# Linear attention and two expert layers: the first batch in a written-out order, its key subtractions and value copies on GpSimd

## The chip, the core and the metric

The kernel runs on one core of a Trainium2 chip. The metric is the device time of one execution in microseconds (us). TensorE (PE) multiplies matrices, VectorE (DVE) and ScalarE (ACT) work on whole tiles, GpSimd (POOL) too, and SyncE (SP) issues the transfers between the chip's main memory and the core's.

## What is computed

```python
# q, k, v: 4 batches x 8 heads x 576 tokens x 64, float32
q_s = exp(q - max over the 64);      q_s = q_s / (sum over the 64 + 1e-09)
k_s = exp(k - max over the tokens);  k_s = k_s / (sum over the tokens + 1e-09)
kv  = einsum("bhsd,bhse->bhde", k_s, v)
att = einsum("bhsd,bhde->bhse", q_s, kv)          # -> x: 2304 tokens x 512
# first expert layer (weights in 64-bit floats)
x   = ((x @ w1) * (x @ w2)) @ w3 @ w_out          # 512 -> 1024 -> 1024 -> 512
# second: 4 experts, weighted by normalised probabilities
out = sum over e of p[:, e] * (relu(x @ e1[e]) @ e2[e])
```

## The kernel before

The tokens run in chunks of 512 columns, `chunks[0]` to `chunks[4]`; a batch has 576 tokens, so chunk 0 is the first 512 tokens of batch 0 and the other 64 belong to chunk 1. The eight heads of a batch are worked in four pairs, in the order `PAIRS = [0, 2, 1, 3]`.

**Attention of one batch.** `load_k`, `load_v`, `load_q` issue the transfers; a pair's keys are a 128x512 tile and a tail of 64 rows. `k_max` takes the maximum over the tokens: three passes on VectorE, a transpose on TensorE, a reduction on VectorE, a matmul that spreads the result over the partitions, and ScalarE's copy `mx`. `k_exp` subtracts `mx` on VectorE (L270) and takes the exponential on ScalarE (L273). `k_v` multiplies keys and values (five matmuls, L285) and makes the block diagonal `bd` of two heads: GpSimd fills it with zeros (L281), ScalarE writes the two blocks, scaled by the reciprocal sums (L299). `load_v` of batch 0 brings the values into a staging tile `vs`, and ScalarE copies them into `vt`, which has a column of ones (L214). The queries come in two tiles `j` of 18 groups of 64: `q_exp` (maximum L308, subtraction L323, exponential L327 with the reordering of rows and heads; for tile (1,1), in `ON_SCALAR`, 18 exponentials of 64 columns with the subtraction and the sum in them, L316), `q_norm` (sum L340, reciprocal, product L343), `q_turn` (three transposes and a copy, three times). `x_stage` multiplies a pair's transposed queries by `bd` in two halves of 288 columns (L368) and splits the result into a high and a low part: ScalarE's copy L384, a matmul with the negative identity L385, ScalarE's copy L389.

**Layer 1.** `ab_step(c, f)`, f from 0 to 7, makes 256 of the 1024 columns of both products of chunk c: two sums of twelve matmuls 128x512 each (three to a pair: high times high L113, high times low L114, low times high L115), called step f below (of chunk 0). The weights come as 64-bit floats and are converted on the chip, one job for each f: two absolute values on ScalarE (`conv_abs`, L144), four passes 128x1024 on VectorE (`conv_rest`, L148, L151, L155, L159), then for each half of the job a high part by a copy on ScalarE (L107) and a low part by a subtraction on VectorE (L108). After that come products of w3 and w_out (`unit`), the rest of the first expert layer, and the second.

**What sets the order.** A scheduler places each engine's instructions. The program gives it the order of the calls: `slot(s)` runs what `put` has listed for slot s by the tables `K_SLOT` and `Q_SLOT` (for batch 0 all in slots 0 to 5; `ab_step(0, f)` is in slot 6 + f). `hold` and `AFTER_JOB` add orders of their own: ("k", 1, 0): 2 means that the first key maximum of batch 1 stands behind the conversion of job 2. SyncE issues all transfers in one row. Psum banks come in pools of two, so a sum has to be read out before the next but one of its pool may start. `keep_busy` issues matmuls that compute nothing needed; the counts behind each pair's transpose, spread and products are `FILL_T`, `FILL_B` and `FILL_V`.

## Time and profile before

| | us |
|---|---|
| median of 3 runs (lowest, highest) | 1153.62 (1153.06, 1154.74) |
| the profiled execution, span from first to last instruction | 1152.2 |
| TensorE busy in it | 1131.9 (98%) |
| VectorE busy | 871.4 (76%) |
| ScalarE busy | 538.3 (47%) |
| GpSimd busy | 50.5 (4%) |

For the profiled execution the span is what is shown; its own time, with what lies around the span, isn't printed beside it. All times in the rows count from the start of the span. The shares are means over 1152 us; the part that the change rewrites is the start, so it is to be read in windows of some microseconds there, engine by engine. An engine's line in a view gives the start, the length, the engine, the line of the code, the operation, out<-in, the size, and in brackets the idle time before it and what ended it. The granted clock (PEclk) is a share of 2.4 GHz.

### The profile page before, as it was taken

How to read it: one execution, taken by the hardware profiler on the slowest of the kernel's cores; microseconds unless marked ns; L12 is line 12 of the kernel's file. 1: busy time of each engine (PE TensorE's matmuls, PEld its weight loads, DVE VectorE, ACT ScalarE, POOL GpSimd, SP SyncE). 2: the span in 40 equal slices, each digit the busy share in tenths (PEclk: the TensorE clock that was granted, in tenths of full speed). 3: DMA queues.
4: the chain of work that ended last, by engine and by line, in shares of the span. 5: the costliest groups of instructions: out<-in, count | busy, mean ns of one | idle time of the engine just before them, and what ended most of it. 6: DMA issues, size and time to landing. Idle time of an engine off the chain costs nothing.

```text
span 1152.2 us, 18837 instructions
## 1 busy us (share of the span) xinstructions
PE 1131.9 (98%) x7091; PEld 1051.2 (91%) x7091; DVE 871.4 (76%) x1432; ACT 538.3 (47%) x986; POOL 50.5 (4%) x74
## 2 busy tenths in 40 slices
PE   7999999999999999999999999999999999999998
PEld 5677877888878889999999999999999999999998
DVE  6986888776558435999989987777779877777777
ACT  4775335755345325655545543334336344344441
POOL 0000032323000000000000000000000000000000
PEclk7999999999999999999999999999999999999999
DMA  9986980899889866877877889777777797777774
GB/s 260 269 330 241 308 203 11 229 323 376 314 290 398 335 261 250 290 284 281 298 265 289 280 313 301 252 246 253 254 249 258 244 307 252 248 246 260 246 247 133
DMA packets 124666, 308.02 MB, mean 267 GB/s; under 512 B 27936, under 2 KB 51488, under 8 KB 124576
## 3 DMA queue, kind: packets, MB, share of 16 engines
q1 hardware_dynamic: 123616, 306.04, 78.2%
q8 instruction: 56, 0.92, 0.3%
q10 hardware_dynamic: 960, 0.79, 0.3%
q14 instruction: 34, 0.28, 0.1%
HBM read 230.24 MB, written 76.55 MB: 266 GB/s over the span
## 4 chain that ended last, share of the span: by engine, by line
PE 88%; DVE 4%; DMA 4%; issue 1%; ACT 1%; SPq 1%; DVEq 0%; ACTq 0%
PE hp L933 30%; PE op L1010 29%; PE ab L113 5%; PE ab L114 5%; PE ab L115 5%; PE y L113 3%; PE y L114 3%; PE y L115 3%; DMA vt<-in_v_dram 2%; PE kv L285 2%; PE xp L368 1%; DMA kr<-in_k_dram 1%; PE W L113 1%; PE W L115 1%; PE W L114 1%
## 5 line engine op out<-in xcount | busy, mean ns | idle before, releaser
L1010 PE MATMUL op<-eg,h 128*128 128x256 f32 x3024 | 379.8, 280 | 0.0
L933 PE MATMUL hp<-t,eg 128*128 128x384 f32 x2016 | 376.6, 336 | 0.9 <-DVE acc L991 0.9
L1010 PEld LDWEIGHTS op<-eg,h 128*128 128x128 f32 x3024 | 373.5, 188 | 0.4 <-PE hp L933 0.3
L933 PEld LDWEIGHTS hp<-t,eg 128*128 128x128 f32 x2016 | 344.6, 188 | 2.5 <-DVE acc L991 1.8
L991 DVE SCALAR_TENSOR_TENSOR acc<-op,prob,acc 128x256 f32<-128x256 f32 (+1 forms) x399 | 197.3, 522 | 42.0 <-PE op L1010 41.9
L107 ACT ACTIVATE h<-blk 128x768 fp32r<-128x768 f32 x168 | 137.9, 842 | 142.3 <-DVE blk L630 108.4
L108 DVE TENSOR_TENSOR h<-blk,h 128x768 fp32r<-128x768 f32 x168 | 156.9, 949 | 24.4 <-ACT h L107 24.3
L916 ACT ACTIVATE blk<-hp 128x384 f32<-128x384 f32 x192 | 90.5, 489 | 142.4 <-PE hp L933 138.9
L920 DVE TENSOR_TENSOR blk<-hp,blk 128x384 f32<-128x384 f32 x144 | 79.1, 554 | 67.7 <-PE hp L933 67.2
L113 PE MATMUL ab<-x,wg 128*128 128x512 f32 (+1 forms) x320 | 120.1, 379 | 2.5 <-ACT bd L299 1.3
L114 PE MATMUL ab<-x,wg 128*128 128x512 f32 (+1 forms) x320 | 118.8, 371 | 0.4 <-ACT x L389 0.4
L115 PE MATMUL ab<-x,wg 128*128 128x512 f32 (+1 forms) x320 | 118.6, 373 | 0.0
L922 ACT ACTIVATE blk<-blk 128x768 f32<-128x768 f32 x72 | 60.6, 845 | 72.7 <-DVE blk L920 71.2
L630 DVE TENSOR_TENSOR blk<-blk 128x768 f32<-128x768 f32 x96 | 91.2, 950 | 0.5
L113 PEld LDWEIGHTS ab<-x,wg 128*128 128x128 f32 x320 | 60.1, 189 | 14.5 <-ACT bd L299 1.7
L114 PEld LDWEIGHTS ab<-x,wg 128*128 128x128 f32 x320 | 60.4, 189 | 11.6 <-ACT x L389 1.9
L115 PEld LDWEIGHTS ab<-x,wg 128*128 128x128 f32 x320 | 60.4, 189 | 10.0
L108 DVE TENSOR_TENSOR eo<-e2r,eo 128x512 fp32r<-128x512 f32 x56 | 41.8, 755 | 21.2 <-ACT eo L107 20.9
L524 DVE TENSOR_TENSOR ah<-ab,ah 128x512 f32<-128x512 f32 (+1 forms) x40 | 25.2, 631 | 39.4 <-PE ab L115 39.2
L114 PE MATMUL y<-h,W 128*128 128x512 f32 x128 | 50.6, 398 | 0.0
L115 PE MATMUL y<-h,W 128*128 128x512 f32 x128 | 50.0, 393 | 0.0
L113 PE MATMUL y<-h,W 128*128 128x512 f32 x128 | 48.9, 402 | 0.0
(103 smaller groups left out, 1060.6 us busy)
## 6 DMA issues: line engine op xcount, KB each, us to landing
eg<-e_t SPq DMA_DIRECT2D x96, 512.0 KB, 4.8
eg<-e_b SPq DMA_DIRECT2D x72, 512.0 KB, 5.2
eg<-e_s SPq DMA_DIRECT2D x68, 512.0 KB, 4.5
eg<-e_a SPq DMA_DIRECT2D x51, 512.0 KB, 4.7
wg<-w SPq DMA_DIRECT2D x44, 512.0 KB, 8.0
f<-in_moe_w_dram SPq DMA_DIRECT2D x32, 512.0 KB, 6.3
e_t<-eo SPq DMA_DIRECT2D x32, 512.0 KB, 7.1
e_s<-eg SPq DMA_DIRECT2D x28, 512.0 KB, 4.3
```

The costliest lines, as they stand in the source:

```text
L107: i = nc.scalar.activation(out=hi, in_=src, func=ACTF.Copy)
L108: j = eng.tensor_tensor(out=lo, in0=src, in1=hi.bitcast(F32), op=ALU.subtract)
L113: nc.tensor.matmul(out=ps, lhsT=w_hi, rhs=r_hi, start=first, stop=False, **kw)
L114: nc.tensor.matmul(out=ps, lhsT=w_hi, rhs=r_lo, start=False, stop=False, **kw)
L115: return nc.tensor.matmul(out=ps, lhsT=w_lo, rhs=r_hi, start=False, stop=last, **kw)
L630: return lambda: nc.vector.tensor_tensor(out=dst, in0=x, in1=y, op=op)
L916: nc.scalar.activation(out=block(name)[:, u], in_=src, func=func)
L920: nc.vector.tensor_tensor(out=x[:, u], in0=src, in1=x[:, u], op=ALU.add)
L922: nc.scalar.activation(out=x, in_=x, func=ACTF.Relu)
L933: nc.tensor.matmul(out=q, lhsT=w[:, sw, kt, P * u:P * u + P], rhs=t[b][:, kt, st], start=new and kt == 0 and i == 0, stop=kt == 1 and i == ...
L991: nc.vector.scalar_tensor_tensor(out=dst, in0=src, scalar=prob[:, T, e:e + 1], in1=dst, op0=ALU.mult, op1=ALU.add,)
L1010: nc.tensor.matmul(out=q[:, c:c + DH], lhsT=g[:, sh, u, P * i:P * i + P], rhs=w[:, sw, u], start=new and u == 0 and j == 0, stop=u == 1 an ...
```

## The change

Batch 0 leaves the tables: its part of `K_SLOT` and `Q_SLOT` is empty, and two new functions write it out. `load_first` issues its transfers: the four key tiles with one transfer of all key tails (`kx`) behind the first, the queries, the values, the values' tails, two jobs of weights. `head` calls small functions (`top`, `spread`, `rest`, `key`, ...) one step at a time, and `seq(engine, inst)` ties each instruction to the one before it on its engine, so that the order is the order of writing. In it

- the subtraction of `mx` from a 128x512 key tile and the copies of the values are on GpSimd (`spread`, `value`); the tails' subtraction stays on VectorE (`rest`);
- the block diagonal is one pass on VectorE, scaled by the reciprocal sum and masked by a tile `same` of zeros and ones (`block`), in place of a fill and two copies on ScalarE;
- queries are exponentiated in place, and the product that normalises them writes them reordered (`norm`); there is one tile `qe`, as before. The same holds for the query tiles of the later batches, (1,1) aside;
- x of chunk 0 is made in matmuls of 512 columns (`out_of`), and the 64 columns of chunk 1 go to one bank `xr` and are split later, behind slot 6 (`x_rest`);
- the conversions of job 0 and the absolute values of job 1 are part of the row (`a_first`, `b_first`), and job 1's four passes are tied to VectorE's row.

Fillers: 78 in place of 43, of which 44 stand behind the last pair's spread. Five jobs are loaded before slot 0. In `AFTER_JOB` batch 1's four keys and its first query tile stand one job earlier. The core of the diff:

```diff
-V_WHOLE = (0,)
-FILL_T, FILL_B, FILL_V = (5, 3, 3, 12), (0, 3, 3, 0), (0, 0, 0, 0)
-K_SLOT = [[0, 0, 0, 0], [6, 7, 8, 9], [30, 32, 34, 36], [46, 47, 48, 50]]
-Q_SLOT = [[2, 2], [6, 8], [30, 34], [46, 48]]
+FILL_T, FILL_B = (5, 3, 3, 3), (0, 3, 3, 44)
+K_SLOT = [[], [6, 7, 8, 9], [30, 32, 34, 36], [46, 47, 48, 50]]
+Q_SLOT = [[], [6, 8], [30, 34], [46, 48]]
 AFTER_JOB = {
-    ("k", 1, 0): 2, ("k", 1, 1): 3, ("k", 1, 2): 4, ("k", 1, 3): 5, ("q", 1, 0): 2, ("q", 1, 1): 3,
+    ("k", 1, 0): 1, ("k", 1, 1): 2, ("k", 1, 2): 3, ("k", 1, 3): 4, ("q", 1, 0): 1, ("q", 1, 1): 3,
     ("in", 2): 13,
 }
...
-        qx = ap_.tile([P, QR, 2, D], F32, tag="qe", name="qe")
-        nc.scalar.activation(
-            out=qx.rearrange("p r h d -> p h r d"), in_=t.rearrange("p (h r) d -> p h r d", h=2),
-            func=ACTF.Exp,
-        )
-        qe[b, j] = qx
+        nc.scalar.activation(out=t, in_=t, func=ACTF.Exp)
+        qe[b, j] = t
...
+    def seq(eng, inst):
+        if eng in chain:
+            after_inst(inst, chain[eng])
+        chain[eng] = inst
+        return inst
...
+            x = kr[i][:, :, 0:KR]
+            seq(G, nc.gpsimd.tensor_tensor(
+                out=x, in0=x, in1=mx.to_broadcast([P, 2, KR, D]), op=ALU.subtract
+            ))
...
+        def value(i):
+            seq(G, nc.gpsimd.tensor_copy(out=vt[0, PAIRS[i]][:, :, 0:KR, 0:D], in_=vs[i]))
...
+            seq(V, nc.vector.scalar_tensor_tensor(
+                out=bd.rearrange("p (h d) -> p h d", h=2),
+                in0=ps[:, 0:2 * D + 2].rearrange("p (h d) -> p h d", h=2)[:, :, 0:D],
+                scalar=rs, in1=same.rearrange("p (h d) -> p h d", h=2),
+                op0=ALU.mult, op1=ALU.mult,
+            ))
...
+            seq(T, nc.tensor.matmul(
+                out=ps, lhsT=st[i]["bd"], rhs=qT[hp % 2][:, hp // 2, 0:CH], start=True, stop=True
+            ))
...
+        top(0), spread(0)
+        top(1), rest(0), key(0)
+        top(2), spread(1)
+        top(3), rest(1), spread(2), spread(3), rest(2), rest(3)
+        key(1), key(2)
+        less(0), query(0), key(3)
+        less(1), query(1)
+        value(0), value(1), value(2), value(3)
+        kv(0), kv(1)
+        total(0), block(0), kv(2), norm(0)
+        total(1), block(1)
+        a_first(0)
+        turn(0, 0), turn(0, 1), kv(3), turn(0, 2)
+        norm(1)
+        out_of(0), out_of(1), out_rest(0), out_rest(1)
+        block(2), block(3), b_first(0)
+        high(0), turn(1, 0), minus_high(0), high(1), turn(1, 1), low(0), minus_high(1)
+        turn(1, 2), low(1)
+        out_of(2), out_of(3), out_rest(2), out_rest(3)
+        high(2), minus_high(2), b_first(1), high(3), minus_high(3), b_first(2)
+        low(2), low(3), a_first(1)
...
-    for i in range(AB0):
-        if i == 3:
-            convert(1)
-        slot(i)
+    load_first()
+    head()
+    load_to(1 + AHEAD)
     for i in range(AB0):
         slot(i)
+    put(after, AB0, x_rest)
```

The order of three places, word for word (a row is the line, the operation, out<-in, the size and how many in a row). First ScalarE, where the steps 3 and 4 of layer 1 are served; before, `wg_736` and `wg_739` are the high parts of step 4's weights, `mx_678` is the maximum of batch 1's third pair, and L316 are the 18 exponentials of query tile (1,1):

```order
L107 ACTIVATE wg_634<-f32_545 128x512
L107 ACTIVATE wg_637<-f32_545 128x512
L523 ACTIVATE ah_680<-ab_681 128x512
L260 ACTIVATE mx_678<-mt_673 128x128
L107 ACTIVATE wg_736<-f32_627 128x512
L107 ACTIVATE wg_739<-f32_627 128x512
L144 ACTIVATE f32_729<-f64_472 128x512 x2
L316 ACTIVATE qe_643,qs_644<-qr_461,qm_640 128x64 x18
L299 ACTIVATE bd_709<-kv_711,rs_717 64x64 x2
```

Now (step 4's are `wg_746` and `wg_749`, the third pair's maximum is `mx_688`, the exponentials are L296, the key exponentials L255):

```order
L761 ACTIVATE ah_690<-ab_772 128x512
L337 ACTIVATE qT_618<-qt_629 128x2x192
L296 ACTIVATE qe_653,qs_654<-qr_455,qm_650 128x64 x18
L255 ACTIVATE ek_673<-kr_447 128x2x4x64
L255 ACTIVATE ek_673<-kr_447 64x128
L242 ACTIVATE mx_688<-mt_683 128x128
L106 ACTIVATE wg_746<-f32_637 128x512
L106 ACTIVATE wg_749<-f32_637 128x512
L279 ACTIVATE bd_719<-kv_721,rs_727 64x64 x2
```

The 18 exponentials stand ahead of the high parts of step 4's weights and of the third maximum, behind which they stood before.

Second VectorE, where it goes from batch 0's queries to the weights of job 0. Before (`f32_324` is job 0, `f32_327` job 1, `qe_258` the second query tile):

```order
L148 TENSOR_SCALAR f32_327<-f32_327 128x1024
L159 SCALAR_TENSOR_TENSOR f32_324<-f64_134,f32_324 128x1024
L295 RECIPROCAL rs_294<-rs_294 128x1
L151 TENSOR_SCALAR f32_327<-f32_327 128x1024
L340 TENSOR_REDUCE qs_345<-qe_258 128x18
L292 TENSOR_SCALAR rs_307<-kv_301 128x1
L155 SCALAR_TENSOR_TENSOR f32_327<-f64_312,f32_327 128x1024
L108 TENSOR_TENSOR wg_334<-f32_324,wg_334 128x512
L108 TENSOR_TENSOR wg_337<-f32_324,wg_337 128x512
L341 TENSOR_SCALAR qs_345<-qs_345 128x18
```

Now (job 0 is `f32_332`; `qe_359` the second query tile, `bdg_150` holds the block diagonals, `kv_316` and `kv_346` are the third and fourth pair's products):

```order
L529 TENSOR_TENSOR qe_359<-qr_123,qs_326 128x2x9x64
L488 TENSOR_SCALAR rs_368<-kv_316 128x1
L491 RECIPROCAL rs_368<-rs_368 128x1
L493 SCALAR_TENSOR_TENSOR bdg_150<-kv_316,rs_368,bdg_150 128x128
L488 TENSOR_SCALAR rs_372<-kv_346 128x1
L491 RECIPROCAL rs_372<-rs_372 128x1
L493 SCALAR_TENSOR_TENSOR bdg_150<-kv_346,rs_372,bdg_150 128x128
L147 TENSOR_SCALAR f32_332<-f32_332 128x1024
L150 TENSOR_SCALAR f32_332<-f32_332 128x1024
L154 SCALAR_TENSOR_TENSOR f32_332<-f64_144,f32_332 128x1024
L158 SCALAR_TENSOR_TENSOR f32_332<-f64_144,f32_332 128x1024
L107 TENSOR_TENSOR wg_413<-f32_332,wg_413 128x512
```

Jobs 0 and 1 stood between the query's passes; now the query's and the blocks' passes are done first, and job 1 comes after job 0's low parts.

Third TensorE, up to layer 1's first matmul (L113 before, L112 now). Before:

```order
L355 MATMUL qt_362<-ident_75,qe_253 128x128 x3
L355 MATMUL qt_367<-ident_75,qe_253 128x128 x3
L355 MATMUL qt_372<-ident_75,qe_253 128x128 x3
L368 MATMUL xp_393<-qT_361,bd_260 128x288
L285 MATMUL kv_301<-vt_148,ek_245 128x130 x5
L368 MATMUL xp_408<-qT_361,bd_273 128x288
L368 MATMUL xp_395<-qT_361,bd_260 128x288
L368 MATMUL xp_410<-qT_361,bd_273 128x288
L385 MATMUL xp_393<-x0_0_397,nident_76 128x288
L385 MATMUL xp_395<-x0_0_397,nident_76 128x224
L113 MATMUL ab_514<-x0_0_397,wg_334 128x512
```

Now:

```order
L560 MATMUL xr_365<-qT_335,bdg_150 128x64 x2
L541 MATMUL qt_383<-ident_75,qe_359 128x128 x3
L572 MATMUL xp_361<-x0_0_380,nident_76 128x512
L541 MATMUL qt_391<-ident_75,qe_359 128x128 x3
L572 MATMUL xp_363<-x0_2_389,nident_76 128x512
L541 MATMUL qt_398<-ident_75,qe_359 128x128 x3
L551 MATMUL xp_404<-qT_382,bdg_150 128x512
L551 MATMUL xp_406<-qT_382,bdg_150 128x512
L560 MATMUL xr_365<-qT_382,bdg_150 128x64 x2
L572 MATMUL xp_404<-x0_1_410,nident_76 128x512
L112 MATMUL ab_507<-x0_0_380,wg_413 128x512
```

The matmuls of 288 columns have become some of 512 and 64, the first matmuls of all four pairs' x stand ahead of the first `ab`, and the transposes of the second query tile (`qe_359`) are among them; before they stood behind it.

## Rows read from the trace of the kernel before

**Rows 1.** Page, head and part 1: span; busy time, share, instructions.

```profile
span 1152.2 us, 18837 instructions
...
PE 1131.9 (98%) x7091; PEld 1051.2 (91%) x7091; DVE 871.4 (76%) x1432; ACT 538.3 (47%) x986; POOL 50.5 (4%) x74
```

**Rows 2.** Windows: length, busy PE, PEld, DVE, ACT, POOL (instructions), PEclk, DMA share, GB/s.

```profile
10.00:20.00 10.00, 6.43 (x30) 4.88 (x30) 5.66 (x11) 3.45 (x6) 0.00 (x0) 0.66 1.08 281
20.00:30.00 10.00, 8.18 (x33) 6.39 (x34) 9.90 (x19) 7.76 (x18) 0.97 (x3) 0.67 1.11 336
...
40.00:50.00 10.00, 8.86 (x43) 6.30 (x42) 10.00 (x20) 8.38 (x22) 0.41 (x2) 1.00 1.15 253
50.00:60.00 10.00, 10.00 (x49) 8.24 (x48) 10.00 (x19) 5.36 (x13) 0.00 (x0) 1.00 1.11 356
```

**Rows 3.** Timeline, TensorE: start, length, line, operation; idle before, releaser.

```profile
10.74 0.49 PE L127 MATMUL busy<-ones 128*128 128x256 bf16 x3
...
14.71 2.77 PE L127 MATMUL busy<-ones 128*128 128x256 bf16 x12
...
22.16 4.71 PE L285 MATMUL kv<-vt,ek 128*128 128x130 f32 x20 [1.80 <-ACT vt L214]
26.80 2.38 PE L355 MATMUL qt<-ident,qe 128*128 128x128 f32 x9
...
33.81 0.51 PE L113 MATMUL ab<-x,wg 128*128 128x512 f32 x1 [0.22 <-ACT bd L299]
...
48.01 0.39 PE L115 MATMUL ab<-x,wg 128*128 128x512 f32 x1
...
69.12 0.39 PE L115 MATMUL ab<-x,wg 128*128 128x512 f32 x1
...
69.80 0.39 PE L115 MATMUL ab<-x,wg 128*128 128x512 f32 x1
...
75.28 1.47 PE L285 MATMUL kv<-vt,ek 128*128 128x130 f32 x10
...
83.06 0.45 PE L113 MATMUL ab<-x,wg 128*128 128x512 f32 x1
```

**Rows 4.** Windows of 1 us, TensorE alone: length, busy, PEclk, DMA share, GB/s.

```profile
23.00:24.00 1.00, 1.00 (x5) 0.65 1.10 348
24.00:25.00 1.00, 0.98 (x5) 0.50 1.10 348
...
30.00:31.00 1.00, 1.00 (x9) 0.93 1.05 175
```

**Rows 5.** Lines by form, VectorE, 0 to 140 us: busy, mean ns | idle before.

```profile
L270 DVE TENSOR_TENSOR kr<-kr,mx 128x512 f32<-128x512 f32 x8 | 5.4, 677 | 0.0
L343 DVE TENSOR_TENSOR qe<-qe,qs 128x1152 f32<-128x1152 f32 x4 | 5.4, 1347 | 0.0
...
L245 DVE TENSOR_TENSOR mf<-m 128x128 f32<-128x128 f32 x8 | 2.2, 281 | 0.1
```

**Rows 6.** ScalarE: lines by form, then the timeline.

```profile
L107 ACT ACTIVATE wg<-f 128x512 fp32r<-128x512 f32 x26 | 15.0, 628 | 2.5 <-DVE f L159 2.3
...
64.68 1.14 ACT L107 ACTIVATE wg<-f 128x512 fp32r<-128x512 f32 x2
...
66.85 0.33 ACT L316 ACTIVATE qe<-qr,qm 128x64 f32<-128x64 f32 x1
...
72.50 0.33 ACT L316 ACTIVATE qe<-qr,qm 128x64 f32<-128x64 f32 x1
```

**Rows 7.** GpSimd: lines by form, then the timeline.

```profile
L270 POOL TENSOR_TENSOR kr<-kr,mx 128x512 f32<-128x512 f32 x8 | 11.9, 1486 | 47.1 <-ACT mx L260 47.1
...
150.87 2.23 POOL L323 TENSOR_TENSOR qr<-qr,qm 128x1152 f32<-128x1152 f32 x1 [43.61 <-DMA vt<-in_v_dram]
...
166.91 4.58 POOL L323 TENSOR_TENSOR qr<-qr,qm 128x1152 f32<-128x1152 f32 x1 [7.30 <-DVE qm L308]
```

**Rows 8.** VectorE: timeline, the first key maximum.

```profile
3.59 0.42 DVE L241 TENSOR_TENSOR m<-kr 128x256 f32<-128x256 f32 x1 [2.46 <-DMA kr<-in_k_dram]
```

276 lines of the change are left out of this document (222 added, 54 removed).

## The prediction, made before the changed kernel was run

> **What bounds the kernel now.** I read the page's busy shares first [rows 1]: TensorE is busy in 98% of 1152.2 us. Nearly all of the change lies in the first 130 us, and beyond them TensorE is the engine that is always busy, so whatever the start gains or loses is carried to the end one for one, and the question is when layer 1's work starts and how tightly it runs in its first steps. The 10 us windows [rows 2] show that stretch: TensorE is busy 6.4 us of 10 to 20, 8.2 of 20 to 30, 8.9 of 40 to 50 and full only from 50 us; VectorE is busy 5.7 us, 9.9, 10.0 and 10.0 in the same windows. So **from 20 us on the bound is VectorE**, and until 50 us TensorE waits for what it makes. The timeline of TensorE [rows 3] gives the dates. Layer 1's first matmul starts at 33.81. A step f is 24 matmuls of 128x512 that come every 0.23 us when nothing is missing (every third one is a line L115: 69.12 and 69.80), 5.5 us in all. Step 0's last is the one at 48.01, step 3's that at 69.80; step 4 is over when the values' products start at 75.28, and step 5 starts at 83.06, after 7.8 us of key, value and query work of batch 1.
>
> **How I add up.** I laid out the rows of both orders, each instruction starting when its engine, its inputs and its buffer were free, with lengths of rows of this trace; for the kernel before this puts step 5 at 82.4 where the trace has 83.06, so sums below are good to about 0.7 us. The trace's own span is 1152.2 us, 1.4 us less than the median of 1153.62, and I take that 1.4 us as unchanged.
>
> **The change part by part.** *Keys.* Eight DMAs for the keys become five, one of them all tails; the first maximum, at 3.59 [rows 8], keeps its date, since the first key tile still comes first. VectorE loses four subtractions of 0.68 us [rows 5], 2.7 us; GpSimd takes them at 1.49 us each (it did eight such subtractions later on) [rows 7], 6.0 us, in a stretch in which it had 0.00 us of work [rows 2]. In the layout they end at 8.7, 11.8, 13.3 and 14.8 us. The last one is on the way to the fourth exponential, not to the first; GpSimd at 1.3 times its length costs 0.4 us, at 2.05 times, as its query subtraction shows (2.23 and 4.58 us for the same shape) [rows 7], 5.9 us.
>
> *Values.* Four copies leave ScalarE. No row has a copy of that size on GpSimd. Bounds: from 0.6 us (ScalarE's pass over 128x512, 0.63) [rows 6] to 2.2 us (1.5 times GpSimd's subtraction of that size). I take 1.0, between ScalarE's pass and GpSimd's subtraction of 1.49, which reads two inputs. Anything from 0.6 to 1.5 moves nothing, because the exponentials of the keys end later; 2.2 alone costs up to 1 us. The four copies end at 19.4, and the products of keys and values start at 16.5.
>
> *Queries and blocks.* A block diagonal, before a fill on GpSimd and two copies on ScalarE, becomes one masked multiplication of 128x128 on VectorE: no row has it, 0.23 to 0.4 us from the 0.28 of a 128x128 maximum [rows 5], I take 0.25, four are 1.0 us. VectorE's two maxima, two subtractions, two sums and two products of 1.35 us each [rows 5] stay, now written with the reordering in the product rather than in ScalarE's pass. The second product waits 1.5 us for the transposes of the first, since there is one such buffer. Total for VectorE: 2.7 saved, 1.0 added, and some 3 us of waits in a fixed row of work in which nothing may step forward. Then job 0's conversion, 27.6 to 31.5, and the first low half of the weights at 33.0.
>
> *x of chunk 0.* Eight matmuls of 288 columns become four of 512 and four of 64, and eight passes on ScalarE of 288 and less become eight of 512 (0.63 us, 128x512) [rows 6]; the 64 rest columns are converted within step 0's shadow. TensorE waits for keys and weights there, so it costs nothing, unless the clock goes (below).
>
> *Fillers.* 43 become 78, of which 44 stand between the last spread of maxima and the first product. At the full clock they take 0.11 us apiece (half of the 0.23 of 512 columns; the three at 10.74 are over in 0.49 us) [rows 3], 4.8 us, and are over at 16.4, when the first product can start anyway: nothing. At half the clock they take 0.23 apiece, as the twelve at 14.71 with their 2.77 us [rows 3]; if the full clock is there only from 18.3, the layout gives +3.0.
>
> *Where that leads.* Layer 1's first matmul: 33.0, against 33.81. Step 0, which waited for x and conversions until 48.3 before, ends at 39.0, since x's parts and both halves of its weights are there together: **9.3 us early**. But job 1's absolute values stand at the end of ScalarE's row, behind the last low part of x, so VectorE waits for them until 36.3 and converts job 1 until 41.2, with pieces of job 2 in between. VectorE was full there and stays full: the total of its work is 1.7 us less, and 3 us of waits are new. So the lead melts: step 1 ends 4.9 us early, step 2 3.9, step 3 **3.4 us early** (66.6 against 70.0).
>
> *Step 4.* Here the order of ScalarE is different, as the fence on ScalarE shows. Before, the copies that make the high halves of step 4's weights stand ahead of the 18 exponentials of query tile (1,1); the copies ran at 64.68, the exponentials from 66.85 to 72.83 [rows 6], 6.0 us, beside steps 3 and 4. Now the exponentials, two key exponentials and a maximum stand ahead of those copies. In the layout the exponentials run 65.4 to 71.7, the keys' two and the maximum (1.0 us together) to 72.7, and the first copy lets step 4 begin at 73.4. TensorE has 1.4 us of key and value work from 66.6, then waits some 5 us; it waits for the maximum besides, which frees a bank. Step 4 ends at 81.0 in place of 75.3, 5.7 late. The work that stood between steps 4 and 5 has by then been done, so that gap is 4.3 us for 7.8: step 5 starts at 85.3, **2.3 us late**. The remaining order of batches 2 and 3 differs in some forty places up to 350 us; laid out that adds 1.3 us by layer 1's last steps. Sum: -0.8 (start) -2.6 (steps 0 to 3 together, to -3.4) +9.1 (step 4's end) -3.4 (gap) +1.3 = **+3.6 us**, 1157.2.
>
> **The rivals.** *B, the start is slower still: the clock or GpSimd.* In the trace the granted clock falls to 0.65 in 23 to 24 us, after TensorE had idled 1.80 us up to 22.16, stays at 0.50 (1.2 of 2.4 GHz) and is back at 0.93 in 30 to 31 [rows 3, 4], though TensorE is busy in all of these windows. After the change the fillers stand in that idle time, but from 21 us on TensorE still waits for VectorE several times. A fall between 23.4 and 30 costs 3.1, cold fillers 3.0, both 5.1; GpSimd at 1.6 times 2.1. These are costs at the end, by the layout, so B is A +3.1: 1160.3, up to 1163. The Trainium skill, in "TensorE: Matmul & The Clock Gate", Part 4, says that transposes in TensorE's transpose mode don't count as its being busy in the same way, so that the full clock doesn't engage on them; by that rule B would be likelier, since fifteen or more transposes stand in that stretch. The trace agrees so far that the clock stayed at half through the nine transposes at 26.80 [rows 3, 4]. And "GPSIMD Engine Reference", section 1, says that GpSimd shares its interface to the memory with VectorE and contends with instructions of two inputs; the 4.58 us beside 2.23 [rows 7] agrees, and by it VectorE's tail subtractions and maxima would lengthen GpSimd's keys.
>
> *C, nothing to be measured.* The exponentials start at 62.2 in the layout, as soon as their input, the negated maxima from VectorE, is there, rather than at 65.4 behind a transpose's copy, and the maximum behind them moves with them: step 4 then ends 3.2 us earlier than in A, the wait of 5 us is less than half, and 1157.2 - 3.2 is 1154.0. For it: lengths in the layout are means, and a date that is off by 3 us is within what 30 us of chained work can add up to. Against it: the layout of the kernel before was off by 0.7 us only.
>
> *D, the other side, faster.* The lead of 3.4 us survives. This needs ScalarE's 18 exponentials to be over before TensorE comes to step 4, that is 5 us earlier relative to step 3's end; the point is a start at 60 in place of 65.4. ScalarE has the room (5.36 us busy of 50 to 60) [rows 2], and then step 4 follows step 3 and the end is 3.4 early: 1150.2. Against it: ahead of them in ScalarE's row stands the copy of a transpose from the middle of step 3, and their input is there at 62.2 only; VectorE would have to be 2 us faster as well.
>
> **How the numbers follow.** A 0.50, with most of it at 1156 to 1158.5; B 0.24, to 1163; C 0.14, 1152.5 to 1155.5 with the bounds of the other prices; D 0.12, 1149.5 to 1151.5. The likeliest is A, 1157.2 us. Differences below 0.2%, 2.3 us (1151.3 to 1155.9), are what a measurement of this kernel can't tell from none. Same: C and the 0.07 of A that falls below 1155.9, together 0.21. Faster: D, 0.12. Slower: the other 0.43 of A and B's 0.24, 0.67. The range leaves out D and a small tail beyond B: 1152 to 1163; A's own is 1156 to 1158.5.
>
> **What will show it.** Right: GpSimd's first work in 7 to 19 us with subtractions of about 1.5 us; layer 1's first matmul near 33.0 and step 0 over by 39 to 40; VectorE full from 36 to 72; a hole of 4 to 6 us on TensorE between step 3 and step 4, ended by ScalarE's copies for the weights or its maximum; step 5 at 85. Wrong: step 4 that follows step 3 within 2 us (D), a granted clock at half between 23 and 31 us (B), subtractions on GpSimd of over 2 us (B), or a first matmul after 36.

## The result and the profile after

The changed kernel takes **1165.57 us** (median of 4 runs, 1165.27 to 1166.05), the kernel before, beside it, 1153.51 (1153.06 to 1154.74). The ratio is 1.0103, 95% interval [1.0089, 1.0117]: slower by 12 us. The forecast had the sign and the places; the size, 3.6 us, was a third of it, and the time lies above the range.

The head of the page after, as [rows 1]:

```profile
span 1164.2 us, 18876 instructions
...
PE 1137.9 (98%) x7122; PEld 1056.2 (91%) x7122; DVE 869.2 (75%) x1432; ACT 532.4 (46%) x966; POOL 54.7 (5%) x81
```

The span has grown by 12.0. TensorE is 6.0 us busier, with the same products to make. Most of that is the fillers, busy 14.46 us now (78) for 9.96 before (43), 4.5 us more. The half clock is hardly more in sum: over windows of 1 us up to 360, busy share times the missing share of the clock adds up to 7.3 us now and 6.1 before (an estimate from the rows); it has moved, from 13 to 31 us to places behind 47. The other 6 us are idle time. The 10 us windows, as [rows 2], show where:

```profile
10.00:20.00 10.00, 9.07 (x57) 7.35 (x58) 7.04 (x14) 3.83 (x10) 7.24 (x10) 1.00 1.08 273
20.00:30.00 10.00, 8.29 (x59) 6.67 (x56) 7.82 (x16) 4.38 (x9) 1.30 (x6) 1.00 1.10 346
...
40.00:50.00 10.00, 6.45 (x26) 4.66 (x25) 8.94 (x12) 4.58 (x13) 0.00 (x0) 0.88 1.12 303
50.00:60.00 10.00, 10.00 (x36) 8.01 (x37) 10.00 (x19) 5.72 (x11) 0.00 (x0) 0.78 1.06 383
...
70.00:80.00 10.00, 6.50 (x29) 5.06 (x29) 10.00 (x22) 9.84 (x45) 0.14 (x1) 0.75 0.55 177
```

VectorE, the bound from 20 us on before, did 9.90 us of work in 20 to 30 then and does 7.82 now, though over the whole span it is busy only 2.2 us less (869.2 for 871.4): its written-out row waits. The price is paid in 40 to 50 and in 70 to 80, where TensorE is busy 6.5 us of ten and its granted clock falls. The timeline of TensorE, as [rows 3], has the dates:

```profile
38.14 0.40 PE L112 MATMUL ab<-x,wg 128*128 128x512 f32 x1
...
43.61 0.39 PE L114 MATMUL ab<-x,wg 128*128 128x512 f32 x1
46.69 0.50 PE L112 MATMUL ab<-x,wg 128*128 128x512 f32 x1 [2.69 <-ACT wg L106]
...
70.72 0.39 PE L114 MATMUL ab<-x,wg 128*128 128x512 f32 x1
...
76.48 0.48 PE L234 MATMUL mt<-ident,mf 128*128 128x128 f32 x1 [2.87 <-DVE f L158]
77.00 0.79 PE L112 MATMUL ab<-x,wg 128*128 128x512 f32 x1
...
86.64 0.40 PE L114 MATMUL ab<-x,wg 128*128 128x512 f32 x1
...
91.78 0.45 PE L112 MATMUL ab<-x,wg 128*128 128x512 f32 x1
...
186.98 0.50 PE L112 MATMUL W<-wg 128*128 128x512 f32 x1 [1.39 <-DVE ah L762]
```

| | before | forecast | after |
|---|---|---|---|
| first `ab` of layer 1 | 33.81 | 33.0 | 38.14 |
| step 0 over | 48.4 | 39.0 | 44.0 |
| step 3 over | 70.0 | 66.6 | 71.0 |
| first and last of the 18 exponentials start | 66.85, 72.50 | 65.4, – | 69.48, 75.12 |
| step 4 begins, ends | 70.0, 75.3 | 73.4, 81.0 | 77.0, 86.9 |
| step 5 begins | 83.06 | 85.3 | 91.78 |
| a pass `ah` (VectorE, L524, now L762) late in layer 1 | 343.51 | +3.6 | 355.12 (+11.6) |

The last row is my yardstick below, called **the lag**. Behind it both kernels run alike: TensorE is busy 779.08 us of 360 to 1140 before and 779.01 after. Between executions of one kernel the timed total scatters by some 6 us on the chips of the experiments, so a date in the trace tells more than a total; but a trace is one execution, and where the clock decides (below) it is not always the usual one. Runs whose head of the program is the same have their first `ab` anywhere from 37.1 to 38.1, so less than 1 us isn't read from one trace.

GpSimd and VectorE at the start, timelines, as [rows 7] and [rows 8]:

```profile
8.63 1.69 POOL L449 TENSOR_TENSOR kr<-kr,mx 128x512 f32<-128x512 f32 x1 [6.86 <-ACT mx L445]
...
14.82 2.65 POOL L449 TENSOR_TENSOR kr<-kr,mx 128x512 f32<-128x512 f32 x2 [0.61 <-ACT mx L445]
17.41 3.40 POOL L473 COPY vt<-vs 128x512 f32<-128x512 f32 x4
```

```profile
5.86 0.28 DVE L428 TENSOR_TENSOR mf<-mf,kx 64x128 f32<-64x128 f32 x1 [1.50 <-DMA kx<-in_k_dram]
...
9.23 1.24 DVE L426 TENSOR_TENSOR mf<-m 128x128 f32<-128x128 f32 x1
...
14.78 0.28 DVE L456 TENSOR_TENSOR kx<-kx,mx 64x128 f32<-64x128 f32 x1 [1.15 <-ACT mx L445]
15.84 0.49 DVE L456 TENSOR_TENSOR kx<-kx,mx 64x128 f32<-64x128 f32 x1 [0.78 <-ACT mx L445]
16.26 1.34 DVE L506 TENSOR_REDUCE qm<-qr 128x18 f32<-128x1152 f32 x1
...
29.91 1.36 DVE L529 TENSOR_TENSOR qe<-qr,qs 128x1152 f32<-128x1152 f32 x1 [1.83 <-PE qt L541]
...
37.95 0.69 DVE L107 TENSOR_TENSOR wg<-f,wg 128x512 fp32r<-128x512 f32 x1 [1.53 <-ACT wg L106]
```

GpSimd's prices were right (1.3 to 1.7 us a subtraction, 0.85 a copy). What wasn't foreseen here stands on VectorE: a wait of 1.50 for the one transfer of all tails, a pass of 0.29 us that takes 1.24 beside GpSimd's subtraction of 8.63, and waits for `mx` that hold up the queries. Those could run: their four transfers are issued from 3.7 to 5.7 us and land 6.0 to 8.1 us after that. The first query pass starts at 16.26, 3.8 us later than in my layout.

ScalarE ahead of step 4, as [rows 6], and the end of job 4's conversion on VectorE:

```profile
69.48 0.34 ACT L296 ACTIVATE qe<-qr,qm 128x64 f32<-128x64 f32 x1
...
75.12 0.34 ACT L296 ACTIVATE qe<-qr,qm 128x64 f32<-128x64 f32 x1
...
75.45 0.82 ACT L255 ACTIVATE ek<-kr 128x512 f32<-128x512 f32 x2
76.17 0.26 ACT L242 ACTIVATE mx<-mt 128x128 f32<-128x128 f32 x1
76.33 1.14 ACT L106 ACTIVATE wg<-f 128x512 fp32r<-128x512 f32 x2
```

```profile
70.73 1.21 DVE L158 SCALAR_TENSOR_TENSOR f<-f,f 128x1024 int32<-128x1024 int32 x1
```

Job 4 is converted at 71.9; the copies that let step 4 begin run 4.4 us later, behind the exponentials, as forecast.

### The profile page after: what moved, and what is told of

Read it like the earlier page. It is cut to its first block, busy times and chain, and to the rows that moved or that the text cites. A ratio compares the mean times of both kernels' runs of the same rounds, so it can differ in the third digit from the quotient of the medians.

```text
span 1164.2 us, 18876 instructions
## 1 busy us (share of the span) xinstructions
PE 1137.9 (98%) x7122; PEld 1056.2 (91%) x7122; DVE 869.2 (75%) x1432; ACT 532.4 (46%) x966; POOL 54.7 (5%) x81
## 4 chain that ended last, share of the span: by engine, by line
PE 84%; DVE 7%; DMA 6%; issue 1%; ACT 1%; SPq 1%; DVEq 0%; POOL 0%; POOLq 0%; ACTq 0%
PE hp L1163 28%; PE op L1240 27%; PE ab L112 5%; PE ab L113 5%; PE ab L114 5%; PE y L112 3%; PE y L113 3%; PE y L114 3%; PE kv L267 1%; DMA vt<-in_v_dram 1%; DMA qr<-in_q_dram 1%; DVE acc L1221 1%; PE xp L348 1%; DMA f<-in_moe_w_dram 1%; PE W L112 1%
## 5 line engine op out<-in xcount | busy, mean ns | idle before, releaser
L1150 DVE TENSOR_TENSOR blk<-hp,blk 128x384 f32<-128x384 f32 x144 | 79.3, 556 | 67.1 <-PE hp L1163 66.6
L112 PE MATMUL ab<-x,wg 128*128 128x512 f32 (+1 forms) x320 | 121.1, 381 | 3.5 <-ACT wg L106 3.0
L113 PE MATMUL ab<-x,wg 128*128 128x512 f32 (+1 forms) x320 | 119.7, 375 | 0.0
L868 DVE TENSOR_TENSOR blk<-blk 128x768 f32<-128x768 f32 x96 | 91.4, 952 | 0.5
L112 PEld LDWEIGHTS ab<-x,wg 128*128 128x128 f32 x320 | 61.0, 191 | 15.9 <-ACT wg L106 4.4
L113 PEld LDWEIGHTS ab<-x,wg 128*128 128x128 f32 x320 | 61.1, 191 | 10.5 <-ACT x L369 0.3
L762 DVE TENSOR_TENSOR ah<-ab,ah 128x512 f32<-128x512 f32 (+1 forms) x40 | 25.3, 633 | 40.6 <-PE ab L114 39.8
L113 PE MATMUL y<-h,W 128*128 128x512 f32 x128 | 50.5, 396 | 0.0
L112 PE MATMUL y<-h,W 128*128 128x512 f32 x128 | 48.2, 400 | 0.0
```

What stands on the lines that cost most here:

```text
L112: nc.tensor.matmul(out=ps, lhsT=w_hi, rhs=r_hi, start=first, stop=False, **kw)
L113: nc.tensor.matmul(out=ps, lhsT=w_hi, rhs=r_lo, start=False, stop=False, **kw)
L868: return lambda: nc.vector.tensor_tensor(out=dst, in0=x, in1=y, op=op)
L1150: nc.vector.tensor_tensor(out=x[:, u], in0=src, in1=x[:, u], op=ALU.add)
```

## The experiments

My theory after the result: the lag begins in VectorE's fixed row, is made larger by the exponentials ahead of step 4's weights, and larger again by the clock that falls behind the waits. The traces bear out the second and third part, though no total shows them by themselves; the first doesn't stand as it is said here (below, the rows taken off). Rivals: GpSimd contends; the fillers; the order of the later batches; the line of `AFTER_JOB`.

**The 18 exponentials behind the high copies** (of step 4's weights).

```diff
-                split(g[:, 0], g[:, 1], ms[n][:, i])
+                hi, _ = split(g[:, 0], g[:, 1], ms[n][:, i])
+                if n == 4:
+                    for late in gate["sc"]:
+                        after_inst(late, hi)
```

> One edit to the changed kernel: the 18 exponentials of query tile (1,1) are ordered behind the two ScalarE copies that make the high halves of step 4's weights. Theory (the wait at step 4 is ScalarE's order plus the half clock that follows it): in the changed kernel those copies could run from 71.9, when VectorE has job 4 converted, but ran at 76.33; step 4 then starts at about 72.7 instead of 77.0, at the full clock, and is over at 78.3 instead of 86.9; step 5 starts at 86 to 87 instead of 91.8, as the exponentials end 3.6 us later; total 1160 to 1161, 5 us less. Rival (VectorE bounds this stretch, and the order on ScalarE only decides where the wait stands): the wait moves to between steps 4 and 5, and step 5 stays at 91 to 92, total 1165 to 1166.

1.0103 [1.0072, 1.0134], lag +9.0 for +11.6. Step 4 follows step 3 (71.92 to 78.7), and yet step 5 comes at 88.83: the exponentials now start at 72.29 and end when step 4 ends, and what needs them stands between steps 4 and 5. ScalarE and TensorE in that run:

```profile
71.23 1.15 ACT L106 ACTIVATE wg<-f 128x512 fp32r<-128x512 f32 x2 [1.31 <-DVE f L158]
72.29 0.33 ACT L296 ACTIVATE qe<-qr,qm 128x64 f32<-128x64 f32 x1
```

```profile
81.98 0.55 PE L335 MATMUL qt<-ident,qe 128*128 128x128 f32 x3 [0.37 <-ACT mx L242]
...
88.83 0.45 PE L112 MATMUL ab<-x,wg 128*128 128x512 f32 x1
```

So a wait moves, and 2.6 us of 11.6 come back in the trace (0.8 of them at the first `ab`, 37.38), none that the total shows. The copies run 5.1 us earlier than in the changed kernel (71.23 for 76.33), and what holds them now is VectorE's conversion (L158, 1.31 idle). Before the change they ran at 64.68 [rows 6]: the rest, 6.5 us, isn't the order on ScalarE.

**Twelve fillers into the hole of 44 to 46.7** (the edit's working lines).

```diff
+            if c == i == 0 and f == 1:
+                for _ in range(12):
+                    m = nc.tensor.matmul(
+                        out=ps[:, 0:256], lhsT=ones[:, 0:P], rhs=ones, start=True, stop=True
+                    )
+                    after_inst(m, gate["pace"][0])
```

> One edit to the changed kernel: 12 fillers of 256 columns, 1.3 us, stand in TensorE's idle time of 2.7 us between steps 0 and 1 (44.0 to 46.7); no other engine's order changes. Theory (part of the loss is the half clock that follows an idle time, 47.5 to 54 us here): idle time of only 1.4 us is left, the granted clock stays at 1.00, step 1's 24 matmuls take some 2 us less, and as VectorE bounds steps 2 and 3 at most 2 us of it reach the end: 1163.5 to 1165. Rival (the clock costs nothing here since VectorE is late anyway, or falls all the same): 1165.6, within 0.5.

1.0096 [1.0069, 1.0124], lag +9.6. The clock still fell, behind an idle time of 1.37, but the stretch at half was about half as long (48.5 to 51.9 for 47.6 to 54.4). The total can't tell it from the changed kernel.

**The tails in four transfers; then also each pair's reduction behind its own maxima.**

```diff
-            if i == 0:
-                nc.sync.dma_start(out=kx, in_=k[0, :, KR * P:S].rearrange("h p d -> p h d"))
+            nc.sync.dma_start(
+                out=kx[:, 2 * hp:2 * hp + 2],
+                in_=k[0, 2 * hp:2 * hp + 2, KR * P:S].rearrange("h p d -> p h d"),
+            )
...
-        top(1), rest(0), key(0)
-        top(2), spread(1)
-        top(3), rest(1), spread(2), spread(3), rest(2), rest(3)
+        top(1), spread(1), rest(0), key(0)
+        top(2), spread(2), rest(1)
+        top(3), spread(3), rest(2), rest(3)
```

> One edit to the changed kernel: the key tails come in four transfers, each behind its pair's tile as before the change, instead of one transfer of all behind the first tile. Theory (the late start begins with the first tail, 5.86 instead of 4.58 for its maximum, and the fixed row hands the delay on): the first pair's tail maximum is at 4.6 to 4.8, the first spread 1 us earlier, layer 1's first matmul 0.5 to 1 us earlier than 38.14; total 1164.6 to 1165.2. Rival (the later pairs' transfers, one place later each, take it back): the first matmul within 0.3 us of 38.14, total 1165.6.

> Two edits to the changed kernel, both on the first pairs' keys: the tails in four transfers as before the change, and in VectorE's row each pair's reduction stands directly behind its own three maxima, where three of the four stood behind those of the next pair. Theory (the row's first 16 us, 3.8 us later than I had laid it out, are handed on to everything behind): the first query maximum on VectorE starts at 13.5 to 15 instead of 16.26, layer 1's first matmul at 35.5 to 37 instead of 38.14, total 1162.5 to 1164.5. Rival (it is given back, as the rows' later waits are for transfers or for VectorE's own work): the first matmul within 0.7 us of 38.14, total 1165 to 1166.

The first part alone: first `ab` 36.86, 1.0094 [1.0061, 1.0126], lag +11.8, nothing. Both: 36.33, 1.0078 [1.006, 1.0095], lag +9.9, with the first query pass at 14.40, as the theory said. The order of the key steps in the row is worth 1.7 to 1.9 us by the lag and 2 to 3 by the totals, whose intervals overlap; the transfers hardly anything by themselves.

**GpSimd's part undone**: the subtractions back on VectorE; and, on the kernel before, both moves alone.

```diff
-            seq(G, nc.gpsimd.tensor_tensor(
+            seq(V, nc.vector.tensor_tensor(
```

```diff
-            nc.scalar.activation(out=t[:, :, 0:KR, 0:D], in_=x, func=ACTF.Copy)
+            nc.gpsimd.tensor_copy(out=t[:, :, 0:KR, 0:D], in_=x)
...
-            either("e", b, hp).tensor_tensor(
+            (nc.gpsimd if b == r0 == 0 else either("e", b, hp)).tensor_tensor(
```

> One edit to the changed kernel: the four key subtractions of 128x512 are back on VectorE, ahead of the tails' subtraction in its row; the value copies stay on GpSimd. Theory (GpSimd's subtractions cost VectorE about 1 us, 1.24 for a maximum of 0.29 beside one of them, and save it 2.7): the maximum takes 0.29 again, but the row holds 2.7 us more; the first matmul is between 1 us earlier and 1.5 us later than 38.14, total 1165 to 1167. Rival (GpSimd's slow subtractions are why the start is late): the first matmul is 2 us or more earlier, total 1163 or less.

> The kernel before the change with one part of it: the four key subtractions of 128x512 and the four value copies of the first batch are on GpSimd; the scheduler places everything. Theory (GpSimd's work as such is cheap; e8 and e4, which took it away from the changed kernel, moved the time by 1 us or less): step 5 within 1.5 us of 83.06, total 1152.5 to 1155.5. Rival (it slows VectorE's passes beside it by more than the 2.7 us that it takes off): step 5 at 85 or later, total 1156.5 or more.

1.0098 [1.008, 1.0117] (lag +9.5), and 1.0012 [0.9999, 1.0026] (lag -0.2) for GpSimd's work in the kernel before: by itself it is next to nothing. Its step 5 came at 84.91, 1.9 us late, between the theory and the rival; behind it the 1.9 were made up. The values' copies back on ScalarE gave 1.0109 [1.0082, 1.0137], lag +11.6. In the run of GpSimd alone VectorE's passes were lengthened by 1 us and more three times, two of them here beside a pass of the usual length, and the kernel's time doesn't show it:

```profile
5.72 0.29 DVE L245 TENSOR_TENSOR mf<-m 128x128 f32<-128x128 f32 x1
...
7.18 1.38 DVE L245 TENSOR_TENSOR mf<-m 128x128 f32<-128x128 f32 x1
...
9.73 1.37 DVE L270 TENSOR_TENSOR kr<-kr,mx 64x128 f32<-64x128 f32 x1
```

**The rows taken off, and two of their kind.** First all ties of `seq` away, so that the scheduler orders batch 0; then, in the row, job 1's absolute values and first two passes earlier.

```diff
-        if eng in chain:
+        if eng in ():
```

```diff
-        block(2), block(3), b_first(0)
+        block(2), block(3), b_first(0), a_first(1)
...
+        conv_rest(ms[1], raws[1], lambda i: seq("DVE", i), (0, 2))
...
-        low(2), low(3), a_first(1)
+        low(2), low(3)
```

> One edit to the changed kernel: the rows are taken away, on every engine; the steps of the first batch are the same ones (GpSimd's subtractions and copies, the masked blocks, x in 512 columns, the fillers), but the scheduler places them. Theory (the fixed rows' waits on VectorE are what is lost: it is idle 14.8 of the first 50 us, 11.1 before the change, and bounds the steps that follow): the conversion passes of jobs 0 and 1 fill those waits, VectorE is idle 11 to 12 of the first 50 us, the wait of 2.7 us between steps 0 and 1 is gone, step 5 starts 3 to 4 us earlier than 91.8, total 1161 to 1163. Rival (the late start comes from transfers and GpSimd, which stay): step 5 within 1 us of 91.8, total 1165 to 1166.

> One edit to the changed kernel's rows: the absolute values of job 1 stand ahead of x's first copy on ScalarE, where it waited 1.2 us, instead of at the end of its row, and the first two of job 1's four passes stand ahead of job 0's low parts on VectorE, where it waited 1.5 us. Theory (waits in the rows): the waits of 1.53 and 1.37 us on VectorE are used, job 1's weights are ready some 2.7 us earlier, step 1 starts at 44 instead of 46.7 with the clock at 1.00, job 4 is converted at 69 to 70 instead of 71.9, step 5 starts 3 us or more earlier, total 1161.5 to 1163. Rival (VectorE's work as such bounds, not its waits): step 1 is earlier but step 5 within 1 us of 91.8, total 1165 to 1166.

1.0125 [1.0106, 1.0143] and 1.0129 [1.0113, 1.0144], lags +12.4 and +14.8: no better, rather worse. Steps 0 to 4 do come earlier (the last `ab` ahead of step 5 at 73.0 and 75.8 for 86.6), but the exponentials start at 73.1 and 74.3 and step 5 at 91.4 and 93.0. Taking the rows off with the exponentials tied ahead of other work of ScalarE gave 1.0128 [1.0104, 1.0151], lag +16.4; the exponentials started at 73.97, where 68 to 70 was expected. Against my theory: a VectorE that waits less at the start isn't enough. Between steps 4 and 5 stands a second chain (batch 1's second query tile), and step 5 needs both.

Nor does taking the ties away make the first `ab` earlier. Without them VectorE is idle 9.5 us of the first 50 (14.8 with them, 11.1 before the change), its first query pass starts 5 us earlier and job 0 is converted at 30.6 instead of 36.4; the first `ab` is at 37.70 all the same. VectorE's first low half waits there for ScalarE's high copy, which stands behind copies for x:

```profile
11.31 1.33 DVE L506 TENSOR_REDUCE qm<-qr 128x18 f32<-128x1152 f32 x1
...
37.45 0.69 DVE L107 TENSOR_TENSOR wg<-f,wg 128x512 fp32r<-128x512 f32 x1 [3.15 <-ACT wg L106]
```

So a second chain is about as long: the first matmuls of all four pairs' x and the transposes of the second query tile stand ahead of the first `ab`, with ties and without.

**The line of `AFTER_JOB`**: undone, and alone on the kernel before (the same edit the other way round).

```diff
-    ("k", 1, 0): 1, ("k", 1, 1): 2, ("k", 1, 2): 3, ("k", 1, 3): 4, ("q", 1, 0): 1, ("q", 1, 1): 3,
+    ("k", 1, 0): 2, ("k", 1, 1): 3, ("k", 1, 2): 4, ("k", 1, 3): 5, ("q", 1, 0): 2, ("q", 1, 1): 3,
```

> One line of the change undone: batch 1's four keys and its first query tile stand behind the job that they stood behind before the change (2 to 5 and 2, not 1 to 4 and 1); the written-out first batch stays. The scheduler then puts the 18 exponentials of query tile (1,1) on ScalarE directly behind the copies for the weights of steps 2 and 3, ahead of batch 1's key exponentials. Theory (step 5 starts when both step 4, 5 to 6 us before, and the 18 exponentials, 10 to 13 us before, are over, as in the eight runs so far; the earlier keys take the time on VectorE and ScalarE in which the query tile and job 4 would have been done): the exponentials are over by 68 instead of 75.5, step 4 starts at 70 to 73 instead of 77.0, step 5 at 83 to 86 instead of 91.8, total 1157 to 1161. Rival (VectorE is behind in any order, by the late start): step 5 at 89 or later, total 1163 to 1166.

> The kernel before the change with one line of the change alone: batch 1's four keys and its first query tile stand one job earlier. Nothing of the first batch is edited. Theory (this line is a good part of the loss, since it puts key work on VectorE and ScalarE ahead of job 4 and of query tile (1,1)): step 5 starts 2 to 6 us later than 83.06, total 1156 to 1159. Rival (the loss lies in the first batch's rows and the late start): step 5 within 1 us of 83.06, total 1153 to 1154.

Undone 1.0072 [1.0057, 1.0088], lag +9.0; alone 1.0037 [1.0021, 1.0052], lag +2.7. Undone, step 5 came at 88.38, between the theory and the rival. Where these texts, and the sections on the kernel before and the change, say that the keys stand behind those jobs or one job earlier, they read the line wrongly, as I had: with the numbers of before a key maximum is issued ahead of the conversion that it should wait for, so that there is nothing to hold it to, and only with the new numbers is it held. VectorE's maxima of batch 1 in the kernel before start at 35.73, 41.34, 48.08 and 53.49; with the line alone:

```profile
34.69 0.36 DVE L241 TENSOR_TENSOR m<-kr 128x256 f32<-128x256 f32 x1
...
45.61 0.42 DVE L241 TENSOR_TENSOR m<-kr 128x256 f32<-128x256 f32 x1
...
59.57 0.42 DVE L241 TENSOR_TENSOR m<-kr 128x256 f32<-128x256 f32 x1
...
61.04 0.42 DVE L241 TENSOR_TENSOR m<-kr 128x256 f32<-128x256 f32 x1
```

Three of the four are 4, 11 and 8 us **later**. Batch 1's chain, which step 5 waits for, begins with them. With the holds gone in the changed kernel, the keys take job 1's place, and TensorE waits at step 1:

```profile
53.05 0.79 PE L112 MATMUL ab<-x,wg 128*128 128x512 f32 x1 [7.73 <-ACT wg L106]
```

**The later batches' queries in their old form** (reordering in ScalarE's exponential, not in the product).

```diff
-        nc.scalar.activation(out=t, in_=t, func=ACTF.Exp)
-        qe[b, j] = t
+        qx = ap_.tile([P, QR, 2, D], F32, tag="qe", name="qe")
+        nc.scalar.activation(
+            out=qx.rearrange("p r h d -> p h r d"), in_=t.rearrange("p (h r) d -> p h r d", h=2),
+            func=ACTF.Exp,
+        )
+        qe[b, j] = qx
```

> One part of the change undone: the queries of batches 1 to 3 are exponentiated into the reordered tile and normalised in place, as before the change; the written-out first batch stays. Theory (the 3 us that the changed kernel loses between 160 and 340 us, a wait of 1.4 us at 185.6 with the clock at half behind it and two waits at 329 to 331, come with this new form): these waits are as short as before the change, the lag at the end is no larger than at step 5, total 1162 to 1164. Rival (they come with the dates at which those parts begin): the lag still grows by 2 us or more behind step 5, total 1165 to 1167.

1.0076 [1.0061, 1.0091], lag +7.4, of which 7.2 are there at step 5: behind step 5 nothing more is lost, where the changed kernel loses 2.9. One place is 185 to 187, where TensorE waits 1.39 us in the changed kernel and 0.78 in this one, and the clock falls only in the first. Of the 1.5 us that this run is ahead at step 5, 1.0 is there at the first `ab` already (37.12), which the edit doesn't touch.

**Twelve fillers for 44.**

```diff
-FILL_T, FILL_B = (5, 3, 3, 3), (0, 3, 3, 44)
+FILL_T, FILL_B = (5, 3, 3, 3), (0, 3, 3, 12)
```

> One number of the change: 12 fillers instead of 44 behind the last pair's spread; only TensorE's row differs. Theory (the fillers cost nothing, since VectorE is busy with the queries until 23 anyway, and keep the clock): the products of keys and values start at 18.3 to 19 instead of 20.85, layer 1's first matmul stays within 0.7 us of 38 or comes later because the clock falls, total 1165 to 1168. Rival (they hold the products up): the first matmul is 1 to 2.5 us earlier, total 1163 to 1164.5.

1.0100 [1.0081, 1.0119], lag +10.7, no difference. The granted clock now is at half in 23 to 29, exactly where rival B had put its fall, and no cost shows (first `ab` 38.17 for 38.14): TensorE is busy for all of these 6 us, where in the changed kernel it waited for part of them.

**Together.** First the old line, the old queries and the early keys (the three edits above); then the last two with the new line kept; that with the exponentials behind the copies; and that with the keys' subtractions on VectorE.

> The changed kernel with the parts undone or mended together: the old table (e9), the old form of the later queries (e13), the key tails in four transfers and each reduction directly behind its own maxima (e7). Theory (the parts add up): 3.6 us from the table, 2.5 from the keys and 2 from the queries leave 3 to 5 of the 12, total 1156.5 to 1159.5. Rival (each of them only moves the same wait of VectorE and ScalarE to another place, so they overlap): total 1161 to 1164.

> The changed kernel with two of the three parts of the last combination undone (later batches' queries in their old form; the key tails in four transfers, each pair's reduction right behind its own maxima), but with the new line of AFTER_JOB kept. Theory 1 (the combination fell short because with the old line nothing holds batch 1's keys, so that one of them stood in VectorE's row ahead of the second query's product and waited for its transfer): here the holds stand, the first ab is at 36.3 to 37.2, and the two gains add up: 4.2 from the queries by the landmark of layer 1's end and 1.7 to 2.6 from the keys, a lag of 5 to 6 there in place of 11.6, a ratio of 1.005 to 1.006. Theory 2 (the parts overlap in the same slack, whatever the holds are): the lag is that of the better one alone, 7 to 7.5, a ratio of 1.007 to 1.0075.

> The same with the 18 exponentials also ordered behind the high copies of step 4's weights. Theory 1 (the hole ahead of step 4 costs mainly by the half clock behind it and by what it shifts, and these come on top of the rest): a further 2 to 2.6 earlier by layer 1's end, as in the first such run, so a lag of 3 to 4. Theory 2 (the wait only moves behind step 4, whatever stands ahead): the lag stays that of the run beside it within 1.

> The kernel of the run before with the four key subtractions back on VectorE (0.68 us each, 2.7 in all); the value copies stay on GpSimd. What is left there is a lag of 3.6 by layer 1's end, of which the first ab, at 37.0 for 33.8, would explain 3.2. Theory 1 (the subtractions on GpSimd hold up the row: they lie beside VectorE's maxima and the exponentials wait for them): the first ab comes at 35.5 to 36.4, a lag of 2 to 3. Theory 2 (VectorE's row pays 2.7 for what it gets back): first ab at 37 to 38, lag 3.5 to 4.5. A ratio near 1.007 in both, within the noise of each other.

| | ratio | first `ab` | step 5 | lag |
|---|---|---|---|---|
| old line, old queries, early keys | 1.0064 [1.0047, 1.0082] | 42.95 | – | +5.3 |
| old queries, early keys | 1.008 [1.0054, 1.0105] | 36.82 | 89.93 | +6.4 |
| and exponentials behind the copies | 1.0089 [1.0061, 1.0117] | 37.01 | 88.45 | +3.6 |
| and subtractions on VectorE | 1.0067 [1.0048, 1.0086] | 36.01 | 89.70 | +8.3 |

In the first, nothing held batch 1's keys, and the scheduler set one into VectorE's row ahead of the second query's product, where it waits for its transfer:

```profile
32.94 0.43 DVE L227 TENSOR_TENSOR m<-kr 128x256 f32<-128x256 f32 x1 [7.03 <-DMA kr<-in_k_dram]
33.28 1.35 DVE L531 TENSOR_TENSOR qe<-qr,qs 128x1152 f32<-128x1152 f32 x1
```

So the new line has a use, to protect the row, and a price; by the total, 1161.19, the rival's range was met, not the theory's. In the next two they nearly add up in the trace (11.6, 6.4, 3.6); the first theories expected 5 to 6 and 3 to 4. In the totals they don't: the third kernel's profiled execution took 1159.25 at a mean granted clock of 0.998, its three others 1163.56 to 1164.05 at 0.990 or 0.991. The last run shows a place where that may be decided. Its first matmul is at the date that was expected without GpSimd's subtractions, 36.01, and its lag is not. Its waits between steps 4 and 5 are the same as the third's within 0.1 us, the longest 0.73 for 0.82, but its clock falls there, here in 1 us windows, TensorE alone, of the last and of the third:

```profile
82.00:83.00 1.00, 0.89 (x6) 0.79 0.08 16
...
85.00:86.00 1.00, 1.00 (x3) 0.50 0.70 135
91.00:92.00 1.00, 1.00 (x4) 0.50 0.87 356
```

```profile
84.00:85.00 1.00, 0.39 (x2) 1.00 0.00 0
85.00:86.00 1.00, 0.99 (x5) 1.00 0.00 0
```

That goes with some 5 us of lag (8.3 for 3.6, with a start 1 us earlier): at half from 82.6 to 92.8, TensorE loses about 4.7 us of work by its windows of 1 us. The first experiment's run had the same row of waits (0.82 the longest) and stayed at the full clock, as the third did. Nothing tried beats the kernel before.

## Why the prediction was wrong

By the steps of the sum, each the change of the lag within its stretch:

| term | forecast | measured |
|---|---|---|
| start: first `ab` | -0.8 | +4.3 |
| steps 0 to 3 | -2.6 | -3.4 |
| step 4's end | +9.1 | +10.7 |
| gap to step 5 | -3.4 | -2.9 |
| later, to the end | +1.3 | +3.3 |
| sum | +3.6 | +12.0 |

**The start was the step that failed.** It was sized at -0.8 and measured +4.3, 5.1 of the miss of 8.4. Each row of VectorE was given its length and its inputs, and the layout for the kernel before was off by 0.7 us; I took that as the error for the new one too. In the changed kernel VectorE's row is late by 3.8 us at its first query pass, by the tails' transfer (the first maximum over at 6.1), the reduction of the second pair behind the third's maxima (10.71), two waits for `mx` ahead of the queries, and a pass of 1.24 for 0.29. By the first low half of the weights it is at 37.95 for 33.0 laid out, 5 us late. Behind it the conversion of job 4 ends at 71.9 (64.1 before), the exponentials start 4.1 us behind the layout, step 4 begins 3.6 behind it.

I had put this down to the tied row, in which a wait can't be filled with other work. The run without ties doesn't bear that out (first `ab` 37.70, the whole run no faster): the first `ab` has a second chain (x and ScalarE's copies) that ends about as late, where the layout had the first `ab` at 33.0. That steps 0 to 4 begin late isn't all of it either, since in that run step 4 was over at 73.4 and step 5 still came at 91.4. Why the start took 5 us longer than laid out is known on VectorE's row only; the cause as a whole stays open. The saving that I had counted on VectorE, 1.7 us, is there (2.2 less busy over the whole span), but four subtractions were never the bound.

**The half clock behind the holes was left out.** The forecast has the hole ahead of step 4 (68.0 to 73.4 there, 72.5 to 77.0 as measured, with a maximum's matmuls in it) and prices it as idle time. TensorE's granted clock after it, and after the two other waits, in 1 us windows (as [rows 4]):

```profile
48.00:49.00 1.00, 0.57 (x3) 0.50 1.06 431
53.00:54.00 1.00, 1.00 (x4) 0.50 1.06 413
...
75.00:76.00 1.00, 0.00 (x0) 0.50 0.92 377
80.00:81.00 1.00, 1.00 (x6) 0.50 0.97 385
...
188.00:189.00 1.00, 1.00 (x3) 0.50 0.00 0
```

Step 4 takes 9.9 us for the 7.6 laid out: 2.3 of the miss of 8.4, beside the 3.6 by which it begins late, 0.5 in the gap and 2.0 later. By the windows of 77 to 82 the half clock takes about 2.4 us of TensorE's work there, which is about the whole of this term. Rival B was right that the start is slower still, and the sign of being wrong, a first matmul after 36, came; neither of B's causes did. No subtraction took over 2 us, and the clock stayed full in 23 to 36, where B looked for a fall:

```profile
23.00:36.00 13.00, 9.75 (x55) 1.00 1.00 271
```

In the run with twelve fillers that fall came, and B's price for it, 3.1 us, didn't.

"TensorE: Matmul & The Clock Gate" of the Trainium skill, Part 4, says that transposes in TensorE's transpose mode don't count as its being busy in the same way. By it the stretch with the fifteen or more transposes was the likely one; here the clock stayed at 2.4 GHz through those from 25.84 to 35 and fell only behind the wait of 2.69 us. That doesn't test the page's statement, since the eighteen transposes are 2.8 of the 9.75 us for which TensorE was busy.

**The later term** was 2 us too small: the new form of the later queries, which I had not priced on its own (the experiment on it gives back 4.2 of the lag, 2.8 of it behind step 5, and 1.0 of the rest is there ahead of the first `ab`).

**The line of `AFTER_JOB`** had no term. I had read the numbers and not what they tie. Alone it costs 0.37%, about 4 us by the total and 2.7 by the lag, partly at the same place as the exponentials, so it can't simply be added.

**Right** were the mechanism ahead of step 4 (exponentials, two key exponentials, a maximum, then the copies), the melting of the lead over steps 1 to 3 (from 4.4 us to a lag of 0.9), GpSimd's prices, the copies that hide, and fillers that cost nothing. D failed as it said it might: a lead needs both the exponentials and VectorE earlier. C was out: the exponentials' input came at 66.3 to 66.5, not at 62.2, and they started at 69.48, behind the copy of a transpose, as A had it. The contention that the Trainium skill's "GPSIMD Engine Reference", section 1, describes (GpSimd shares its interface to the memory with VectorE's two-input instructions) is in the trace, but the forecast looked for it on the wrong side: VectorE's maximum took 1.24 for 0.29, GpSimd's subtractions no more than 1.69. It is on a few passes only, and GpSimd's part as a whole gave 1.0012 [0.9999, 1.0026] in the kernel before.

**What stays open.** Of the lag of 11.6 the runs attribute 3 to 4 to the later queries, 1 to 2 to the keys' order and 2.6 to 2.8 to the exponentials' place, by traces of single executions; the totals don't show that these add up. The rest goes with a first matmul at 36 to 37 for 33.8. Taking the ties away didn't bring it back; how it splits between x of all four pairs ahead of the first `ab`, x in 512 columns and the masked blocks wasn't tried. Why the clock fell in one of three executions with nearly the same waits is open too.

## What to carry to other kernels

That a layout meets the old order within 0.7 us says little of a new one: this one was 5 us off at its first product. And a wait found on the busiest engine isn't yet the cause: before it is called that, take it away and look whether another chain ends as late, as x and ScalarE did here. When a hole on TensorE is foreseen, price the matmuls behind it at half the clock too. And before an entry of a table of holds is called earlier or later, look at whether it ties anything at all.
